# Reordering the first two batches of a linear-attention and swish kernel: fp32 loads of k and q on the hardware queue, one GpSimd queue, and a new order of work around the first Y product

## The chip, the cores and the metric

The kernel runs on one core of a Trainium2 chip. The metric is device time in microseconds (us) of one execution. A core has a matrix engine (TensorE, PE in the profile, with its weight loads listed apart as PEld), a vector engine (VectorE, DVE), an activation engine (ScalarE, ACT), a general engine (GpSimd, POOL) and a queue engine that only issues transfers (SyncE, SP). Each engine runs its own instructions in program order and waits on semaphores for the others. Transfers are issued on SyncE's, ScalarE's or GpSimd's queue; a transfer that changes the type (fp32 in memory to bf16 on chip) is issued by GpSimd.

## The reference

Eight batches of linear attention, then a two-layer feed-forward step over all 4608 rows (8 batches of 576):

```
phi(x) = (x if x > 0 else exp(x) - 1) + 1
kv  = einsum('bhsd,bhse->bhde', phi(k), v)
z   = sum over s of phi(k)
x   = (phi(q) kv) / (phi(q) z + 1e-6)          # (batch, 576, 8 heads * 64)
h   = x @ w_in                                   # 512 -> 2048
g   = h * sigmoid(beta * h)
out = g @ w_out                                  # 2048 -> 512, fp32
```

q, k, v are (8, 8, 576, 64) in fp32, w_in is 512x2048, w_out 2048x512 and beta 2048, all fp32. One batch of q, of k or of v is 1.18 MB, each weight matrix 4.19 MB.

## The kernel before, in words

**The steady part.** From batch 1 on, `h_phase(b)` makes h in 16 blocks of 128 features ("ff"): four 128x512 matmuls (`h_mm`, L334) into one PSUM tile out of four (`mmps`), then one silu on ScalarE (L342) that writes g. `y_phase(b)` multiplies four tiles of 128 rows with w_out (`y_mm`, L352), copies each to SBUF (`y_out`, L364) and stores it. Between the blocks, `at(...)` hangs side work of the next batch on a block's number: `kv_both(n)` (phi(k)^T v, 36 small matmuls, L184), `numer(n, t)` (phi(q) times kv for 128 rows, L285, into the only tile of the pool `numps`, then den, rden and the product xs on VectorE, L293 to L299), and transposes by DMA (`x_trans_dma`, `q_trans_dma`). Products of the last 64 rows of each batch gather in `xT_tail` and are multiplied at the end.

**phi.** `phi_part` takes exp on ScalarE (L149) into a tile "e" that has three buffers; `phi_relu` makes max(x,0)+1 on VectorE (L153) into a tile "r", three buffers too; `phi_min` takes the smaller (L160). Each covers half the heads ("pr" 0 or 1), 1152 columns.

**The first two batches.** The order of work here is written out by hand, and each engine keeps it. Batch 0 has nothing to hide behind: k comes as fp32 by SyncE into `stage`, q and v cast to bf16 by GpSimd; the phi steps are followed by transposes of phi(q) on TensorE (`q_trans0`, copied out of PSUM by ScalarE, through the pool `miscps` with two buffers), `kv_direct` (phi(k)^T v, L195) with its masked copy `kv_evac` (L219), the denominators (`dens`, `recips`, L414 to L422), the products `numer0` (L432) with `norm` (xs, L299), and the transposes `x_trans` (L315) copied into xT by ScalarE (L320) or VectorE (L322). `idle(n)` issues n matmuls on a constant tile. Then come the 16 blocks of h(0), and a stage called Y0 here: the Y product of batch 0, laid between the attention work of batch 1 and the phi of batch 2.

**Weights.** w_in is loaded in four pieces by GpSimd, cast to bf16. w_out is loaded in four fp32 pieces by SyncE into `w_out_f`: pieces 0 and 1 share memory with g of odd batches (`g_sb[1]`, seen as fp32 as `g_f`), pieces 2 and 3 with `stage`, where k of batch 0 lies. `w_out_scale(i, n_act)` (L531 on ScalarE, L533 on VectorE) divides piece i by beta and makes it bf16. `hold(d, after)` makes the issue of one transfer wait until another has landed; pieces 0 and 2 of w_out, k of batch 1 and q of batch 2 are held so.

The lines that matter most for the order are these:

```
e: work.tile(..., tag="e", bufs=3)          # L148
nps: numps.tile(...), pool numps with bufs=1 # L281, L605
y_sb: work.tile(..., tag="y_sb", bufs=3)    # L363
load_w_out(0, w_in_dma[1]); load_w_out(1)    # L119, L120
hold(load(nc.gpsimd, xk[1], k, 1), w_in_dma[3])   # L121
w_out2_dma = load_w_out(2, q1_dma); load_w_out(3) # L458, L459
hold(load(nc.gpsimd, xq[2], q, 2), w_out2_dma)    # L552
```

Of the kernel before, what the change touches and what calls it, by code (L numbers as in the profile page):

```python
# [16 lines left out]
def kernel(  # L17
# [10 lines left out]
    nc = tc.nc  # L28
# [56 lines left out]

    def hold(d, after):
        tc.add_manual_dep(d.ins, after.ins.name, SYNC, reason="share of the queues")


    beta_row = consts.tile([FC, P], F32)  # L90
    for h0 in (0, 2):
        load(nc.sync, k0f, k, 0, h0, 2)
    nc.sync.dma_start(out=beta_row, in_=moe_beta.rearrange("(c p) -> c p", p=P))
    nc.vector.memset(warm, 0.5)  # L94
    tiny = consts.tile([P, 2], BF16)
    nc.scalar.activation(tiny[:, 0:1], warm[:, 0:1], ACTF.Exp)
# [1 line left out]
    make_identity(nc, identity)  # L98
    ident16 = consts.tile([FC, FC], F32)
    make_identity(nc, ident16)  # L100
    for h0 in (0, 2):
        load(nc.gpsimd, xq[0], q, 0, h0, 2)
    for h0 in (0, 2):
        load(nc.gpsimd, vb[0], v, 0, h0, 2)

    w_in_v = moe_w_in.rearrange("(c p) f -> p c f", p=P)
    w_out_v = moe_w_out.rearrange("(c p) m -> p c m", p=P)
    w_in_dma = [
        nc.gpsimd.dma_start(out=w_in_sb[i], in_=w_in_v[:, :, i * 512 : (i + 1) * 512])  # L109
        for i in range(4)  # L110
    ]

    def load_w_out(i, after=None):
        d = nc.sync.dma_start(out=w_out_f[i], in_=w_out_v[:, i * 4 : (i + 1) * 4, :])
        if after is not None:
            hold(d, after)
        return d

    load_w_out(0, w_in_dma[1])  # L119
    load_w_out(1)  # L120
    hold(load(nc.gpsimd, xk[1], k, 1), w_in_dma[3])  # L121
    q1_dma = load(nc.gpsimd, xq[1], q, 1)
    load(nc.gpsimd, vb[1], v, 1)

    kvmask = consts.tile([P, 2, 2, EA], BF16)
    nc.vector.memset(kvmask, 0.0)
    nc.vector.memset(kvmask[:D, :, 0, :], 1.0)
    nc.vector.memset(kvmask[D:P, :, 1, :], 1.0)
    ones = consts.tile([P, 2], BF16)
    nc.vector.memset(ones, 1.0)  # L130
    for i in range(2):
        nc.vector.memset(vaug[i][:, :, :, :, D : D + 2], 1.0)

    warm_ps = mmps.tile([P, 512], F32, tag="mm", name="warm_ps")

# [29 lines left out]
        )  # L165

    def xin(b, a, pr):
        if b == 0 and a == "k":
            return k0f[:, 2 * pr : 2 * pr + 2]
        return (xk if a == "k" else xq)[b % NX][:, 2 * pr : 2 * pr + 2]  # L170

    def v_copy(eng, b, pr):
# [186 lines left out]
    def rows(b, j):  # L359
        return out[b * S : (b + 1) * S, :].rearrange("(g j) m -> j g m", j=J)[j]  # L360

    def y_out(b, t, yp, c0=0, c1=512, queues=(nc.sync, nc.sync)):
        y_sb = work.tile([P, DM], F32, tag="y_sb", name="y_sb", bufs=3)  # L363
        nc.vector.tensor_copy(y_sb[:, c0:c1], yp[:, c0:c1])  # L364
# [77 lines left out]
    def phi_step(a, pr, f, *r):  # L442
        f(0, a, pr, *((xin(0, a, pr),) if f is not phi_min else ()), *r)
# [11 lines left out]
    phi_step("q", 1, phi_part, 0, 4)  # L455
    phi_step("q", 1, phi_part, 4, J)
    phi_step("k", 1, phi_relu)
    w_out2_dma = load_w_out(2, q1_dma)  # L458
    load_w_out(3)  # L459
    phi_step("k", 1, phi_min)  # L460
    zt = [num0_tile() for _ in range(2)]
    z_products(0, 0, zt)
# [9 lines left out]
    z_evac(zt)  # L472
    phi_step("q", 0, phi_min)
    phi_step("q", 1, phi_relu)
    phi_step("q", 1, phi_min, 0, 4)
    phi_step("q", 1, phi_min, 4, J)
    idle(10)

    def q_trans0(t):
        q_trans(0, (t,), misc_bf()[:, 0 : 512 if t < NT - 1 else 256], (nc.scalar,))  # L480

    q_trans0(0)
    q_trans0(1)
    kv_direct(0, 0, kvp0)
    for hh in range(2):
        kv_evac(0, hh, (0,), kvp0)
    q_trans0(2)
    kvp1 = [num0_tile() for _ in range(2)]
    kv_direct(0, 1, kvp1)
    for hh in range(2):  # L490
        kv_evac(0, hh, (1,), kvp1)
    dens(0, (0, 1), dps)
    recips(0, 2, P, dps)
    q_trans0(3)
    numer0(0, 0)
    numer0(0, 1)
# [42 lines left out]
    w_out_scale(0, 0)
    w_out_scale(1, 0)  # L540
    yps = [mm_tile("y_ps") for _ in range(4)]
    phi_all(1, "k")
    phi_all(1, "q")
# [2 lines left out]
            y_mm(0, t, i, yps[t])  # L546
    kv1 = [miscps.tile([P, 512], F32, tag="misc", name="kv1") for _ in range(2)]
    kv_tile(1)
    for pr in range(2):
        z_products(1, pr, kv1)  # L550
    z_evac(kv1)
    hold(load(nc.gpsimd, xq[2], q, 2), w_out2_dma)  # L552
    load(nc.gpsimd, xk[2], k, 2)
    load(nc.gpsimd, vb[0], v, 2)

    for ts in ((0, 1), (2, 3)):
        q_trans(1, ts, num0_tile().bitcast(BF16), (nc.scalar, nc.scalar))
    for pr in range(2):
        kv_direct(1, pr, kv1)
    w_out_scale(2, 0)  # L560
    for hh in range(2):
        kv_evac(1, hh, (0, 1), kv1)
    dps1 = num0_tile()
    q_trans(1, (4,), dps1.bitcast(BF16)[:, 512:768], (nc.scalar,))
    y_mm(0, 0, 2, yps[0])
# [17 lines left out]
    y_mm(0, 1, 3, yps[1])
    y_out(0, 1, yps[1])
    x_trans(1, 3, nc.vector)
    phi_tile(2, "q")
    phi_tile(2, "k")
# [4 lines left out]
    phi_min(2, "q", 0)
    phi_part(2, "k", 0, xin(2, "k", 0))
    y_mm(0, 2, 3, yps[2])
    y_out(0, 2, yps[2])
    phi_min(2, "q", 1)
    phi_part(2, "k", 1, xin(2, "k", 1))
    y_mm(0, 3, 3, yps[3])
    y_out(0, 3, yps[3])
# [89 lines left out]
```

## Time and profile before

| quantity | value |
|---|---|
| time, median of 10 runs | 295.49 us (294.22 to 296.24) |
| the profiled execution's own time | 295.46 us |
| its span (first to last instruction) | 293.7 us |
| TensorE busy | 284.9 us (97%) |
| ScalarE busy | 159.9 us (54%) |
| VectorE busy | 116.5 us (40%) |
| GpSimd busy | 33.7 us (11%) |
| HBM read, written | 36.71 MB, 9.44 MB |

The span leaves out 1.8 us around it, in which the execution starts and ends. The busy share of TensorE is high for a reason beside useful work: matmuls are pipelined and their ends are modelled, and the `idle` matmuls count too. So the gaps of an engine, and who ended them, say more than its share. In the views, a line begins with the start in us and the duration in us, then engine, line, operation, output<-input, and, in brackets, how long the engine had been idle and what ended the idle time.

### The profile page before, as it was taken

Reading aid. Unit: us, or ns where it says so; the run is one execution under the profiler, and the core shown is the slowest. Engines: PE = TensorE matmul, PEld = TensorE weight load, DVE = VectorE, ACT = ScalarE, POOL = GpSimd, SP = SyncE. Lnnn points to the kernel's source line nnn. Section 1 sums busy time; section 2 is a strip of 40 time slices with the busy share of each in tenths; the row PEclk is TensorE's granted clock in tenths of the full one; section 3 lists DMA queues with packets and bytes.
Section 4 is the critical chain, followed back from the end, with each engine's and each line's share of the span. In section 5 each row is a group of like instructions: output and inputs, shape, how many; then the busy total and the mean of one; then the engine's idle time right before and its main releaser. Section 6 shows DMA issues by size and latency. Waiting matters only on the chain.

```text
span 293.7 us, 4697 instructions
## 1 busy us (share of the span) xinstructions
PE 284.9 (97%) x1853; PEld 143.0 (49%) x1881; DVE 116.5 (40%) x266; ACT 159.9 (54%) x208; POOL 33.7 (11%) x50
## 2 busy tenths in 40 slices
PE   8999999999999999999999999999999999999995
PEld 3584456445445444554455445544554444444443
DVE  4753478843724461356135622653251200110012
ACT  5658956855936772678157906690661077018500
POOL 9103020320050005000500053000000000000000
PEclk9999999999999999999999999999999999999999
DMA  7999989789389859952993299416131310131032
GB/s 202 202 213 329 195 291 197 191 250 189 73 223 261 111 53 212 281 85 59 238 250 73 50 234 255 91 35 164 38 71 44 73 37 0 36 74 36 0 71 73
DMA packets 51910, 40.82 MB, mean 139 GB/s; under 512 B 30752, under 2 KB 42288, under 8 KB 51888
## 3 DMA queue, kind: packets, MB, share of 16 engines
q1 hardware_dynamic: 40080, 27.68, 37.2%
q0 software_dynamic: 11648, 12.72, 26.4%
q8 instruction: 14, 0.23, 0.3%
q10 hardware_dynamic: 160, 0.13, 0.2%
q14 instruction: 8, 0.07, 0.1%
HBM read 36.71 MB, written 9.44 MB: 157 GB/s over the span
## 4 chain that ended last, share of the span: by engine, by line
PE 79%; DMA 12%; POOL 2%; DVE 2%; issue 1%; ACT 1%; SPq 0%; POOLq 0%
PE y_ps L352 39%; PE h_ps L334 35%; DMA w_in<-in_moe_w_in_dram 6%; DMA xq<-in_q_dram 3%; PE nps L285 3%; DMA stage<-in_moe_w_out_dram 2%; PE kvp L184 2%; DMA qTd<-phi_q 1%; POOL w_in L109 1%; ACT g L342 1%; POOL xq L81 1%; DVE w_out L533 1%; POOL vf L81 0%; PE nps L432 0%; ACT L342 0%
## 5 line engine op out<-in xcount | busy, mean ns | idle before, releaser
L342 ACT ACTIVATE g<-h_ps,beta_c 128x512 bf16<-128x512 f32 x144 | 98.0, 688 | 100.6 <-PE h_ps L334 100.4
L352 PE MATMUL y_ps<-w_out,g 128*128 128x512 bf16 (+2 forms) x581 | 126.7, 373 | 1.0 <-DVE w_out L533 0.2
L334 PE MATMUL h_ps<-xT,w_in 128*128 128x512 bf16 (+1 forms) x545 | 116.7, 360 | 1.0 <-DVE y_sb L364 0.4
L352 PEld LDWEIGHTS <-g 128*128 128x128 bf16 x592 | 57.4, 98 | 65.7 <-issue 0.8
L334 PEld LDWEIGHTS <-w_in 128*128 128x128 bf16 x624 | 56.6, 98 | 58.9 <-issue 1.0
L364 DVE COPY y_sb<-y_ps 128x512 f32<-128x512 f32 (+2 forms) x37 | 24.9, 675 | 84.5 <-PE y_ps L352 80.9
L299 DVE TENSOR_TENSOR xs<-nps,rden 128x512 bf16<-128x512 f32 (+1 forms) x40 | 27.2, 687 | 4.8 <-DMA xT<-xs 2.4
L81 POOL DMA_DIRECT2D xk<-in_k_dram x7 | 5.4, 771 | 118.7 <-DMA qTd<-phi_q 77.5
L149 ACT ACTIVATE e<-xq 128x1152 bf16<-128x1152 bf16 (+2 forms) x17 | 17.9, 1099 | 1.8 <-DMA xq<-in_q_dram 1.7
L160 DVE TENSOR_TENSOR phi_q<-e,r 128x1152 bf16<-128x1152 bf16 (+2 forms) x17 | 12.2, 722 | 15.9 <-ACT e L149 15.8
L149 ACT ACTIVATE e<-xk 128x1152 bf16<-128x1152 bf16 x14 | 15.5, 1151 | 1.2 <-DVE phi_q L160 1.1
L234 DVE TENSOR_TENSOR kv_bd<-kvp,kvmask 128x260 bf16<-128x260 f32 x12 | 4.6, 424 | 25.8 <-PE kvp L184 25.8
L293 DVE TENSOR_SCALAR den<-nps 128x8 f32<-128x8 f32 (+1 forms) x30 | 5.0, 165 | 23.4 <-PE nps L285 23.4
L334 PE MATMUL h_ps<-xT_tail,w_in 128*128 128x512 bf16 x63 | 13.9, 379 | 0.1
L285 PEld LDWEIGHTS <-qTd 128*128 128x128 bf16 x120 | 9.4, 98 | 7.9 <-DMA qTd<-phi_q 0.8
L160 DVE TENSOR_TENSOR phi_k<-e,r 128x1152 bf16<-128x1152 bf16 x16 | 11.6, 753 | 3.8 <-ACT e L149 3.8
L285 PE MATMUL nps<-kv_bd,qTd 128*128 128x130 bf16 x120 | 12.1, 221 | 1.0 <-DMA qTd<-phi_q 0.6
L174 POOL CAST vaug<-vf 128x1152 bf16<-128x1152 f32 x10 | 11.2, 1161 | 3.6 <-DMA vf<-in_v_dram 3.6
L138 PE MATMUL warm_ps<-warm 128*128 128x512 bf16 x27 | 8.7, 483 | 1.6 <-DVE warm L94 1.5
L149 ACT ACT_TABLE_LOAD x6 | 7.7, 1283 | 2.8 <-DMA xq<-in_q_dram 2.7
L342 ACT ACT_TABLE_LOAD x7 | 9.0, 1283 | 0.1
L81 POOL DMA_DIRECT2D xq<-in_q_dram x9 | 6.8, 755 | 14.5 <-DMA stage<-in_moe_w_out_dram 14.5
(67 smaller groups left out, 104.2 us busy)
## 6 DMA issues: line engine op xcount, KB each, us to landing
out_dram<-y_sb SPq DMA_DIRECT2D x70, 128.0 KB, 2.4
vf<-in_v_dram SPq DMA_DIRECT2D x5, 1152.0 KB, 7.6
xk<-in_k_dram POOLq DMA_DIRECT2D x7, 576.0 KB, 8.6
xq<-in_q_dram POOLq DMA_DIRECT2D x7, 576.0 KB, 12.7
w_in<-in_moe_w_in_dram POOLq DMA_DIRECT2D x4, 512.0 KB, 13.4
g<-in_moe_w_out_dram SPq DMA_DIRECT2D x2, 1024.0 KB, 9.5
stage<-in_moe_w_out_dram SPq DMA_DIRECT2D x2, 1024.0 KB, 7.7
stage<-in_k_dram SPq DMA_DIRECT2D x2, 576.0 KB, 4.3
```

The lines of the kernel that those rows point to most:

```text
L81: return eng.dma_start(out=dst[:, h0 : h0 + n].rearrange("p h j d -> p h (j d)"), in_=rows.rearrange("(i p) e -> p i e", p=P)[:, h0 : h0 + n],
L138: nc.tensor.matmul(warm_ps[:, 0:cols], warm[:, 0:P], warm[:, 0:cols], start=True, stop=True)
L149: nc.scalar.activation(st[b, a, pr, "e"][:, :, j0:j1], x[:, :, j0:j1], ACTF.Exp)
L160: nc.vector.tensor_tensor(st[b, a][:, pr, j0:j1].rearrange("p j (h d) -> p j h d", h=2), st[b, a, pr, "e"][:, :, j0:j1].rearrange("p h j d ...
L174: eng.tensor_copy(vaug[b % 2][:, pr, :, :, 0:D], src[:, 2 * pr : 2 * pr + 2].rearrange("p h j d -> p j h d"),)
L184: nc.tensor.matmul(ps[hh, pr], st[b, "k"][r, pr, j, :], vaug[b % 2][r, pr, j, :, 0:EA], start=(j == 0), stop=(j == J - 1), skip_group_chec ...
L285: nc.tensor.matmul(nps[: qs.shape[-1], hh, pr * 2 * EA : (pr + 1) * 2 * EA], qs, st[b, "kv"][:, hh, pr, :], start=True, stop=True, skip_gr ...
L299: nc.vector.tensor_mul(xs[:n].rearrange("p i a d -> p a i d"), num, rd[:, :, :, None].to_broadcast([n, 2, 4, D]),)
L334: nc.tensor.matmul(hp[:, c0:c1], w_in_sb[ff // 4][:, kc, (ff % 4) * P : (ff % 4 + 1) * P], x[:, kc, c0:c1], start=(kc == 0), stop=(kc == K ...
L342: nc.scalar.activation(g_sb[b % 2][:, ff, :], hp, ACTF.Silu, scale=beta_c[:, ff : ff + 1])
L352: nc.tensor.matmul(yp[:, c0:c1], g_sb[b % 2][:, ff, t * P : (t + 1) * P], w_out_sb[i][:, c, c0:c1], start=(ff == 0), stop=(ff == FC - 1), ...
L364: nc.vector.tensor_copy(y_sb[:, c0:c1], yp[:, c0:c1])
```

## The change

- **Loads of batch 0.** q of batch 0 now comes as fp32 by SyncE behind k, into `g_sb[1]` (`q0f`); its phi reads fp32. beta is issued by ScalarE. v of batch 0 is issued by GpSimd once the first half of k has landed.
- **One GpSimd queue.** All w_out pieces move from SyncE's queue to GpSimd's. The order there is v of batch 0, w_in 0 to 3, w_out 0 to 2, k and q of batch 1, w_out 3, v of batch 1, then q, k, v of batch 2. The four holds named above are gone. The memsets of `kvmask` move from VectorE to GpSimd.
- **Batch 0.** `q_trans0(2)` comes before the first `kv_direct`; `dens` and `recips` of tiles 0 and 1 come before the second.
- **Y0.** The part of w_out piece 2 (`y_mm(0, t, 2)`) is spread between the sums z and the transposes of q of batch 1. Piece 3 of w_out is scaled on VectorE alone, earlier. The copy of y tile 0 goes to ScalarE; the copies of y tiles 1, 2, 3 go behind the last `norm` of batch 1. The exps of q of batch 2 move forward, the other phi steps of batch 2 come after the y copies. `x_trans(1, 1)` is copied by VectorE.
- **h(1).** `x_trans(1, 4)` moves from block 0 to block 5, `kv_both(2)` from 6 to 8; `numer(2, t)` moves from blocks 7, 9, 11, 13, 15 to blocks 10, 11, 12, 13, 14.

```diff
+    q0f = g_f[:, 0 : 4 * J * D].rearrange("p (h j d) -> p h j d", h=4, j=J)
...
-    for h0 in (0, 2):
-        load(nc.sync, k0f, k, 0, h0, 2)
-    nc.sync.dma_start(out=beta_row, in_=moe_beta.rearrange("(c p) -> c p", p=P))
+    nc.scalar.dma_start(out=beta_row, in_=moe_beta.rearrange("(c p) -> c p", p=P))
+    k0_dma, _, _, _ = [
+        load(nc.sync, dst, src, 0, h0, 2) for dst, src in ((k0f, k), (q0f, q)) for h0 in (0, 2)
+    ]
...
-    for h0 in (0, 2):
-        load(nc.gpsimd, xq[0], q, 0, h0, 2)
-    for h0 in (0, 2):
-        load(nc.gpsimd, vb[0], v, 0, h0, 2)
...
-    load_w_out(0, w_in_dma[1])
-    load_w_out(1)
-    hold(load(nc.gpsimd, xk[1], k, 1), w_in_dma[3])
-    q1_dma = load(nc.gpsimd, xq[1], q, 1)
-    load(nc.gpsimd, vb[1], v, 1)
-
-    nc.vector.memset(kvmask, 0.0)
-    nc.vector.memset(kvmask[:D, :, 0, :], 1.0)
-    nc.vector.memset(kvmask[D:P, :, 1, :], 1.0)
+    nc.gpsimd.memset(kvmask, 0.0)
+    nc.gpsimd.memset(kvmask[:D, :, 0, :], 1.0)
+    nc.gpsimd.memset(kvmask[D:P, :, 1, :], 1.0)
...
+    for h0 in (0, 2):
+        hold(load(nc.gpsimd, vb[0], v, 0, h0, 2), k0_dma)
+    for i in range(4):
+        nc.gpsimd.dma_start(out=w_in_sb[i], in_=w_in_v[:, :, i * 512 : (i + 1) * 512])
+    def load_w_out(i):
+        nc.gpsimd.dma_start(out=w_out_f[i], in_=w_out_v[:, i * 4 : (i + 1) * 4, :])
...
-    w_out2_dma = load_w_out(2, q1_dma)
-    load_w_out(3)
...
     phi_step("q", 1, phi_relu)
+    for i in range(3):
+        load_w_out(i)
+    load(nc.gpsimd, xk[1], k, 1)
+    load(nc.gpsimd, xq[1], q, 1)
+    load_w_out(3)
+    load(nc.gpsimd, vb[1], v, 1)
...
-    q_trans0(0)
-    q_trans0(1)
+    for t in range(3):
+        q_trans0(t)
     kv_direct(0, 0, kvp0)
     for hh in range(2):
         kv_evac(0, hh, (0,), kvp0)
-    q_trans0(2)
+    dens(0, (0, 1), dps)
+    recips(0, 2, P, dps)
     kvp1 = [num0_tile() for _ in range(2)]
     kv_direct(0, 1, kvp1)
     for hh in range(2):
         kv_evac(0, hh, (1,), kvp1)
-    dens(0, (0, 1), dps)
-    recips(0, 2, P, dps)
...
+    load(nc.gpsimd, xq[2], q, 2)
+    load(nc.gpsimd, xk[2], k, 2)
+    load(nc.gpsimd, vb[0], v, 2)
     nc.vector.reciprocal(rbeta, beta_c)
-    w_out_scale(0, 0)
-    w_out_scale(1, 0)
+    for i in range(3):
+        w_out_scale(i, 0)
...
     kv_tile(1)
+    y_mm(0, 0, 2, yps[0])
     for pr in range(2):
         z_products(1, pr, kv1)
     z_evac(kv1)
+    w_out_scale(3, 0)
     for ts in ((0, 1), (2, 3)):
         q_trans(1, ts, num0_tile().bitcast(BF16), (nc.scalar, nc.scalar))
+    y_mm(0, 1, 2, yps[1])
+    y_mm(0, 2, 2, yps[2])
+    dps1 = num0_tile()
+    q_trans(1, (4,), dps1.bitcast(BF16)[:, 512:768], (nc.scalar,))
     for pr in range(2):
         kv_direct(1, pr, kv1)
...
+    y_mm(0, 3, 2, yps[3])
+    y_mm(0, 0, 3, yps[0])
+    y_out(0, 0, yps[0], copier=nc.scalar)
     numer0(1, 0)
     numer0(1, 1)
+    phi_tile(2, "q")
+    phi_tile(2, "k")
+    phi_part(2, "q", 0, xin(2, "q", 0))
+    y_mm(0, 1, 3, yps[1])
     x_trans(1, 0, nc.scalar)
     numer0(1, 2)
+    phi_part(2, "q", 1, xin(2, "q", 1))
+    y_mm(0, 2, 3, yps[2], 0, 256)
+    x_trans(1, 1, nc.vector)
     numer0(1, 3)
+    y_mm(0, 2, 3, yps[2], 256, 512)
+    y_mm(0, 3, 3, yps[3], 0, 256)
     x_trans(1, 2, nc.vector)
+    y_mm(0, 3, 3, yps[3], 256, 512)
+    x_trans(1, 3, nc.vector)
     numer0(1, 4)
+    for t in (1, 2, 3):
+        y_out(0, t, yps[t])
     for pr in range(2):
+        phi_part(2, "k", pr, xin(2, "k", pr))
+        phi_relu(2, "q", pr, xin(2, "q", pr))
+        phi_min(2, "q", pr)
     for pr in range(2):
         phi_relu(2, "k", pr, xin(2, "k", pr))
...
         if b == 1:
-            at(sh, 0, lambda: q_trans_dma(2), lambda: x_trans(1, 4, nc.vector))
+            at(sh, 0, lambda: q_trans_dma(2))
+            at(sh, 5, lambda: x_trans(1, 4, nc.vector))
...
-            at(sh, 6 if b == 1 else 4, lambda: kv_both(n))
+            at(sh, 8 if b == 1 else 4, lambda: kv_both(n))
             for t in range(NT):
-                at(sh, (7 if b == 1 else 5) + 2 * t, lambda t=t: numer(n, t))
-                at(sh, min((8 if b == 1 else 6) + 2 * t, FC - 1), lambda t=t: x_trans_dma(n, t))
+                ff = 10 + t if b == 1 else 5 + 2 * t
+                at(sh, ff, lambda t=t: numer(n, t))
+                at(sh, ff + 1, lambda t=t: x_trans_dma(n, t))
```

More of the change, by code (lines that the diff above doesn't have):

```diff
@@ L100 @@
     make_identity(nc, ident16)
-    for h0 in (0, 2):
-        load(nc.gpsimd, xq[0], q, 0, h0, 2)
-    for h0 in (0, 2):
-        load(nc.gpsimd, vb[0], v, 0, h0, 2)
[L106 to L117, printed above, removed]
-    load_w_out(0, w_in_dma[1])
-    load_w_out(1)
-    hold(load(nc.gpsimd, xk[1], k, 1), w_in_dma[3])
-    q1_dma = load(nc.gpsimd, xq[1], q, 1)
-    load(nc.gpsimd, vb[1], v, 1)
     kvmask = consts.tile([P, 2, 2, EA], BF16)
-    nc.vector.memset(kvmask, 0.0)
-    nc.vector.memset(kvmask[:D, :, 0, :], 1.0)
-    nc.vector.memset(kvmask[D:P, :, 1, :], 1.0)
+    nc.gpsimd.memset(kvmask, 0.0)
+    nc.gpsimd.memset(kvmask[:D, :, 0, :], 1.0)
+    nc.gpsimd.memset(kvmask[D:P, :, 1, :], 1.0)
     ones = consts.tile([P, 2], BF16)
@@ L132 @@
         nc.vector.memset(vaug[i][:, :, :, :, D : D + 2], 1.0)
+    for h0 in (0, 2):
+        hold(load(nc.gpsimd, vb[0], v, 0, h0, 2), k0_dma)
+    w_in_v = moe_w_in.rearrange("(c p) f -> p c f", p=P)
+    w_out_v = moe_w_out.rearrange("(c p) m -> p c m", p=P)
+    for i in range(4):
+        nc.gpsimd.dma_start(out=w_in_sb[i], in_=w_in_v[:, :, i * 512 : (i + 1) * 512])
+    def load_w_out(i):
+        nc.gpsimd.dma_start(out=w_out_f[i], in_=w_out_v[:, i * 4 : (i + 1) * 4, :])
     warm_ps = mmps.tile([P, 512], F32, tag="mm", name="warm_ps")
@@ L167, in xin @@
     def xin(b, a, pr):
-        if b == 0 and a == "k":
-            return k0f[:, 2 * pr : 2 * pr + 2]
+        if b == 0:
+            return (k0f if a == "k" else q0f)[:, 2 * pr : 2 * pr + 2]
         return (xk if a == "k" else xq)[b % NX][:, 2 * pr : 2 * pr + 2]
@@ L360, in rows, with y_out @@
         return out[b * S : (b + 1) * S, :].rearrange("(g j) m -> j g m", j=J)[j]
-    def y_out(b, t, yp, c0=0, c1=512, queues=(nc.sync, nc.sync)):
+    def y_out(b, t, yp, c0=0, c1=512, queues=(nc.sync, nc.sync), copier=nc.vector):
         y_sb = work.tile([P, DM], F32, tag="y_sb", name="y_sb", bufs=3)
-        nc.vector.tensor_copy(y_sb[:, c0:c1], yp[:, c0:c1])
+        copy(copier, y_sb[:, c0:c1], yp[:, c0:c1])
         for i in range(2):
@@ L551 @@
     z_evac(kv1)
-    hold(load(nc.gpsimd, xq[2], q, 2), w_out2_dma)
-    load(nc.gpsimd, xk[2], k, 2)
-    load(nc.gpsimd, vb[0], v, 2)
+    w_out_scale(3, 0)
     for ts in ((0, 1), (2, 3)):
         q_trans(1, ts, num0_tile().bitcast(BF16), (nc.scalar, nc.scalar))
+    y_mm(0, 1, 2, yps[1])
+    y_mm(0, 2, 2, yps[2])
+    dps1 = num0_tile()
+    q_trans(1, (4,), dps1.bitcast(BF16)[:, 512:768], (nc.scalar,))
     for pr in range(2):
         kv_direct(1, pr, kv1)
[L560 to L565, printed above, removed]
     dens(1, range(NT), dps1)
@@ L568 @@
     recips(4, 5, G, dps1)
-    y_mm(0, 1, 2, yps[1])
+    for hh in range(2):
+        kv_evac(1, hh, (0, 1), kv1)
+    y_mm(0, 3, 2, yps[3])
+    y_mm(0, 0, 3, yps[0])
+    y_out(0, 0, yps[0], copier=nc.scalar)
     numer0(1, 0)
     numer0(1, 1)
-    w_out_scale(3, 2)
-    y_mm(0, 2, 2, yps[2])
+    phi_tile(2, "q")
+    phi_tile(2, "k")
+    phi_part(2, "q", 0, xin(2, "q", 0))
+    y_mm(0, 1, 3, yps[1])
     x_trans(1, 0, nc.scalar)
     numer0(1, 2)
-    y_mm(0, 3, 2, yps[3])
-    x_trans(1, 1, nc.scalar)
+    phi_part(2, "q", 1, xin(2, "q", 1))
+    y_mm(0, 2, 3, yps[2], 0, 256)
+    x_trans(1, 1, nc.vector)
     numer0(1, 3)
-    y_mm(0, 0, 3, yps[0])
-    y_out(0, 0, yps[0])
+    y_mm(0, 2, 3, yps[2], 256, 512)
+    y_mm(0, 3, 3, yps[3], 0, 256)
     x_trans(1, 2, nc.vector)
+    y_mm(0, 3, 3, yps[3], 256, 512)
+    x_trans(1, 3, nc.vector)
     numer0(1, 4)
[L583 to L587, printed above, removed]
+    for t in (1, 2, 3):
+        y_out(0, t, yps[t])
     for pr in range(2):
-        phi_part(2, "q", pr, xin(2, "q", pr))
-    for pr in range(2):
+        phi_part(2, "k", pr, xin(2, "k", pr))
         phi_relu(2, "q", pr, xin(2, "q", pr))
[L592 to L599, printed above, removed]
+        phi_min(2, "q", pr)
     for pr in range(2):
```

## The prediction

> **What bounds the kernel now.** I read the chain of waits first, then TensorE's timeline for gaps, then the timelines of the engines that end the gaps, then the transfers stretch by stretch. The page gives the shares of busy time and of the chain:
>
> ```profile
> PE 284.9 (97%) x1853; PEld 143.0 (49%) x1881; DVE 116.5 (40%) x266; ACT 159.9 (54%) x208; POOL 33.7 (11%) x50
> PE 79%; DMA 12%; POOL 2%; DVE 2%; issue 1%; ACT 1%; SPq 0%; POOLq 0%
> ```
>
> The chain puts 12% on transfers, all before 62.5 us, so this looks transfer-bound at the front. TensorE's timeline denies it from 16.5 us on: h(0), Y0 and h(1) follow one another with gaps below 0.7 us. I cut the front into stages. Up to 16.54 us (first h0 matmul) VectorE's chain rules; 16.5 to 32.08 is h(0); 32.08 to 52.53 is Y0; 52.53 to 70.53 is h(1) with attention of batch 2. From 70.5 us nothing in the diff touches the program. The hand-over from Y0 to h(1) in ScalarE's timeline is the part to know by heart:
>
> ```profile
> 50.94 1.16 ACT L149 ACTIVATE e<-xk 128x1152 bf16<-128x1152 bf16 x1
> 53.24 1.16 ACT L149 ACTIVATE e<-xk 128x1152 bf16<-128x1152 bf16 x1 [1.15 <-DVE phi_q L160]
> 54.43 1.28 ACT L342 ACT_TABLE_LOAD   x1
> 55.72 3.82 ACT L342 ACTIVATE g<-h_ps,beta_c 128x512 bf16<-128x512 f32 x6
> ```
>
> The fourth exp of batch 2 waited for phi_q: there are three buffers "e", and the fourth tile takes the one that the first `phi_min` has read. Table load and first silu of h(1) stand behind that exp. VectorE's timeline shows how early that min came, with only one y copy between the copy of xT and the relus:
>
> ```profile
> 50.78 0.69 DVE L364 COPY y_sb<-y_ps 128x512 f32<-128x512 f32 x1
> 51.39 0.41 DVE L322 COPY xT<-xtp 128x512 bf16<-128x512 bf16 x1
> 51.73 0.82 DVE L153 TENSOR_SCALAR r<-xq 128x1152 bf16<-128x1152 bf16 x2
> 52.46 0.75 DVE L160 TENSOR_TENSOR phi_q<-e,r 128x1152 bf16<-128x1152 bf16 x1
> ```
>
> And one `numer` of h(1), VectorE's timeline:
>
> ```profile
> 62.89 0.17 DVE L293 TENSOR_SCALAR den<-nps 128x8 f32<-128x8 f32 x1 [1.25 <-PE nps L285]
> 63.09 0.20 DVE L294 RECIPROCAL rden<-den 128x8 f32<-128x8 f32 x1
> 63.33 0.69 DVE L299 TENSOR_TENSOR xs<-nps,rden 128x512 bf16<-128x512 f32 x1
> 64.84 0.17 DVE L293 TENSOR_SCALAR den<-nps 128x8 f32<-128x8 f32 x1 [0.83 <-PE nps L285]
> ```
>
> TensorE ended that product at 62.85; xs ended at 64.02. So the only nps tile is taken for 1.2 us, and the 0.83 us idle shows slack at a distance of two blocks.
>
> **What the Trainium skill says.** "DMA: Bandwidth & Descriptors", section Anatomy of one DMA, prices a GpSimd-issued load at about 2.0 us + bytes/436e3: 2.4 us of moving for a w_out piece (estimate). The trace moves w_in at 205 to 209 GB/s written as bf16, so some 410 read: near it; an fp32-to-fp32 load on that queue is not in it. The same page, section Queues, rings and completion order, has each transfer engine serve its rings in turn. The trace differs; in the stretch 23 to 24 us, with both queues loaded (packets, MB, share):
>
> ```profile
> q1 hardware_dynamic: 176, 0.36, 97.0%
> q0 software_dynamic: 17, 0.02, 9.7%
> ```
>
> The hardware queue took nearly all. "ScalarE: Activation LUTs", section What ACT_TABLE_LOAD costs, gives 1283 ns and a drain of about 1380 ns; the trace shows 1283 ns and the silu 10 ns later, so I charge 1.28.
>
> **Loads.** k and q by SyncE: 2.36 MB at 0.40 MB/us (394 to 406 GB/s at 3 to 5 us), 0.28 of it moved by 3.0 us: ends near 8.2, where q ended at 10.18 before. v is held until 4.46 (first half of k landed), but GpSimd's transfers got almost nothing before 5.4 us anyway: free. Then one queue at 0.41: v and w_in 5.37 MB end at 21.3; w_out 0 to 2 at 29.0; k1 31.9; q1 34.8; w_out 3 37.3; v1 40.2; q2 43.1; k2 46.0; v2 48.8 (before 54.5). GpSimd issues 0.75 us each, two v, four w_in, then w_out from about 11 us when phi has read q0f: always ahead of the queue. Moving the issues off SyncE leaves it only stores. ScalarE's beta issue costs 0.46 us as SyncE's row did, ahead of a table load that ended 2.2 us before the first exp could start; GpSimd's kvmask memsets (0.62 us on VectorE, 0.2 each by GpSimd's own memset rows) lie before k lands. Both cost nothing; past 2.2 us they would delay the first exp or v.
>
> **Ramp.** VectorE works from 4.46 almost unbroken: r(k), min, r(k), min 8.1, beta 8.8. fp32 makes each r(q) 0.76 us (row of `stage`) in place of 0.45: +0.6, which the two waits for exps (0.56 at 9.9 and 0.1 at 11.1) absorb because q is early. Last min of q about 11.95; before 11.97. So the earlier q buys nothing. `q_trans0(2)` now waits in front of `kv_direct` for ScalarE's first copy (two misc buffers; copy 0.58 from 11.9), so `kv_direct` starts 0.5 us later, half of it regained by `dens` running in its shadow: **+0.25**. Bounds: -1.0 (VectorE follows q) to +0.6. h(0) is TensorE's own; Y0 starts at 32.3.
>
> **Y0.** TensorE's sum for the same instructions: 64 y matmuls 13.9, z 0.54, 18 transposes 1.0, kv 1.1, dens 0.6, 20 numer 1.17, 16 transposes 0.9: 19.2 us. Before took 20.45. The new order puts y blocks before each product that waits: w_out 3 lands at 37.3, needed by VectorE near 40.8; v1 at 40.2, needed near 43.4; q2 before 47.6. I keep 0.4 for the last xT copy and small waits: h(1) starts at T = 32.3 + 19.6 = **51.9** (gain 0.6). A transfer over 3 us late reaches TensorE.
>
> **Hand-over.** VectorE after T: norm of tile 4 ends T+0.6; three y copies, 0.62 each: T+2.5; r(q) 0.41, min 0.75: T+3.65. Only then exp k1 (T+3.7 to 4.85), table 1.28, silu 0.69: T+6.85. TensorE has four PSUM tiles: blocks 0 to 3 at 0.864, block 1 waiting 0.45 for y copy 1, end at T+3.9. Block 4 waits for silu 0: **a stall of 2.95 us**, starting block 4 at 58.75. Before, block 3 started at 56.06, block 4 at 56.92. Behind the waiting exp stand table and all silus; behind the y copies all phi of batch 2. qTd (issue after min q1 at about T+4.9, some 6 us to the second landing) comes by 63 and is needed at 66.
>
> **Rest of h(1).** Before, block 4 to the end: 70.53 - 56.92 = 13.61. To add: `x_trans(1,4)` 0.22, now after block 4. The numers stand one block apart: 0.864 us for a tile taken 1.2: stall 0.36, four times, **+1.43**. To subtract: the qTd wait 0.64. Gives 14.62, end at 73.37 against 70.53: +2.84. The profiled 295.46 becomes **298.3**; the median (295.49) is the same within 0.03.
>
> **Rivals.**
> - *Half the loss (12%).* One of the two stalls is hidden: without the nps waits 296.9, without the hand-over's 295.4. Speaks for it that y tile 1 is ready by 48 us; against it that VectorE keeps program order, and that before's exp did wait 1.15 us for its tile. Mostly 296 to 297.
> - *Late transfers (15%).* w_out on GpSimd's queue is unmeasured. Below: at 0.436 MB/us all is 2 us earlier, worth nothing. Above: at half speed each piece costs 2.6 more, v1 lands at 50.6, 7 us after need: 305. At 0.33 MB/us v1 lands near 48 if everything slows (5 us late), at 42.7 if only w_out does: nothing. Value taken: 0.41. Typical of this case: 300 to 303.
> - *The front was transfer-bound (8%), not slower.* The chain's 12% is right, q's 1.9 us and the earlier weights pull the start of h(0). It decides when T is below 49.1: 2.84 earlier than mine. For it: the chain; against: VectorE busy 7.49 of 10 us at 10 to 20, TensorE without gaps after 16.5. T of 48.5 gives 294.9.
>
> **Numbers.** Main case 65%, its own range 297.2 to 299.8; a measurement tells about 0.2% (0.6 us) from no change. Half: 3 of 12 within 0.2%, the rest slower; front: 6 of 8 faster, 2 same. Faster 0.06, same 0.05, slower 0.89. Range 295.9 to 301.8: leaves out the front case and late transfers of the heavy kind.
>
> **To look for after.** ScalarE's fourth exp of batch 2 with a wait of over 3 us for phi_q; the first silu of h(1) near 58; TensorE idle near 3 us before block 4; nps waits of 0.3 to 0.4 for xs, four times; no wait for q at VectorE before 12 us; w_out transfers at about 400 GB/s on the software queue. I am wrong if h(1) starts before 50, if the exp finds a free tile, or if TensorE waits for a transfer in Y0.

## The result, and the profile after

The changed kernel takes 301.41 us (median of 9 runs, 299.73 to 301.79) against 295.21 for the kernel before (32 runs): a ratio of 1.0192, with a 95% interval of 1.0170 to 1.0214. The forecast was slower, 298.3 in a range of 295.9 to 301.8. The direction and the two main waits came as forecast; the size is twice the forecast.

The profiled execution after took 299.73 us with a span of 298.0 (before 295.46 and 293.7), so the profile shows 4.3 us of the loss. The page's shares hardly move; in the chain that ended last the share of transfers falls from 12% to 2%, and TensorE's grows from 79% to 90%:

```profile
PE 285.1 (96%) x1860; PEld 143.6 (48%) x1889; DVE 116.8 (39%) x265; ACT 158.3 (53%) x206; POOL 35.8 (12%) x55
PE 90%; DVE 4%; DMA 2%; ACT 2%; issue 1%; SPq 0%; DVEq 0%
```

By the stages of the forecast, read from TensorE's timeline (us from the start of the span):

| point | before | after | difference grows by |
|---|---|---|---|
| h(0) starts | 16.54 | 17.32 | +0.78 |
| Y0 starts | 32.08 | 32.75 | -0.11 |
| h(1) starts | 52.53 | 52.65 | -0.55 |
| block 4 of h(1) starts | 56.92 | 59.48 | +2.44 |
| Y phase of batch 1 starts | 70.53 | 74.73 | +1.64 |
| end of the span | 293.7 | 298.0 | +0.1 |

**The hand-over.** ScalarE's timeline after, the same four instructions as before:

```profile
50.84 1.15 ACT L138 ACTIVATE e<-xk 128x1152 bf16<-128x1152 bf16 x1
56.27 1.16 ACT L138 ACTIVATE e<-xk 128x1152 bf16<-128x1152 bf16 x1 [4.27 <-DVE phi_q L149]
57.45 1.28 ACT L331 ACT_TABLE_LOAD   x1
58.74 3.58 ACT L331 ACTIVATE g<-h_ps,beta_c 128x512 bf16<-128x512 f32 x6
```

The exp's wait for its buffer has grown from 1.15 to 4.27 us, because on VectorE the three y copies now stand ahead of the first min of q:

```profile
52.53 0.68 DVE L288 TENSOR_TENSOR xs<-nps,rden 64x512 bf16<-64x512 f32 x1
53.13 1.87 DVE L231 COPY y_sb<-y_ps 128x512 f32<-128x512 f32 x3
54.93 0.44 DVE L142 TENSOR_SCALAR r<-xq 128x1152 bf16<-128x1152 bf16 x1
55.47 0.76 DVE L149 TENSOR_TENSOR phi_q<-e,r 128x1152 bf16<-128x1152 bf16 x1
```

TensorE's timeline shows what that costs, and the distance of the numer products. First the kernel before, at block 3 and at two of the numer products:

```profile
56.06 3.61 PE L334 MATMUL h_ps<-xT,w_in 128*128 128x512 bf16 x16 [0.45 <-DVE y_sb L364]
...
64.65 1.89 PE L334 MATMUL h_ps<-xT,w_in 128*128 128x512 bf16 x8
66.37 0.40 PE L285 MATMUL nps<-kv_bd,qTd 128*128 128x130 bf16 x4
```

Then the changed kernel:

```profile
53.86 2.75 PE L323 MATMUL h_ps<-xT,w_in 128*128 128x512 bf16 x12 [0.18 <-DVE y_sb L231]
59.48 1.89 PE L323 MATMUL h_ps<-xT,w_in 128*128 128x512 bf16 x8 [2.87 <-ACT g L331]
...
67.35 1.02 PE L323 MATMUL h_ps<-xT,w_in 128*128 128x512 bf16 x4
68.73 0.41 PE L274 MATMUL nps<-kv_bd,qTd 128*128 128x130 bf16 x4 [0.36 <-DVE xs L288]
```

That is 2.87 us of idling before block 4, and 0.36 us before each of four numer products. The five products stand 1.63 us apart (67.11, 68.73, 70.37, 72.00, 73.63), where their own work and one block take 0.23 + 0.864 us in a row without waits: each wait costs 0.54 us, the idle time and 0.18 more. Most of the 0.18 is seen in the block ahead of the wait: it lasts 1.02 us to its (modelled) end, where in an unbroken row the next work starts 0.864 us after it. This part is called the refill below.

**What the profile doesn't show.** The mean granted clock is the share of full speed that TensorE's clock was let run at, averaged over an execution. Of the ten executions of the changed kernel with a clock on record, four took 299.73 to 300.47 us at a mean granted clock of 0.997 to 0.999, and six 301.41 to 301.79 at 0.992 to 0.994. The profiled one is of the first group, the median of the second: 1.7 us that no view of that profile holds. Runs e1 and e5 below point to where it is lost.

### The profile page after: what moved, and what is told of

Its sections match the earlier page's. It is cut to its first block, busy times and chain, and to the rows that moved or that the text cites. A ratio compares the mean times of both kernels' runs of the same rounds, so it can differ in the third digit from the quotient of the medians.

```text
span 298.0 us, 4712 instructions
## 1 busy us (share of the span) xinstructions
PE 285.1 (96%) x1860; PEld 143.6 (48%) x1889; DVE 116.8 (39%) x265; ACT 158.3 (53%) x206; POOL 35.8 (12%) x55
## 3 DMA queue, kind: packets, MB, share of 16 engines
q1 hardware_dynamic: 38480, 24.65, 34.4%
## 4 chain that ended last, share of the span: by engine, by line
PE 90%; DVE 4%; DMA 2%; ACT 2%; issue 1%; SPq 0%; DVEq 0%
PE y_ps L341 42%; PE h_ps L323 39%; PE nps L274 3%; PE kvp L173 2%; DMA g<-in_q_dram 2%; DVE xs L288 1%; PE nps L421 1%; ACT e L138 1%; PE xtp L304 1%; DVE y_sb L231 1%; DVE phi_q L149 1%; PE kv L184 1%; ACT g L331 0%; ACT L331 0%; PE nps L242 0%
## 5 line engine op out<-in xcount | busy, mean ns | idle before, releaser
L341 PE MATMUL y_ps<-w_out,g 128*128 128x512 bf16 (+3 forms) x588 | 125.9, 370 | 0.8 <-issue 0.2
L341 PEld LDWEIGHTS <-g 128*128 128x128 bf16 x600 | 58.2, 98 | 65.4
L231 DVE COPY y_sb<-y_ps 128x512 f32<-128x512 f32 (+2 forms) x36 | 24.1, 673 | 85.8 <-PE y_ps L341 83.1
L138 ACT ACTIVATE e<-xq 128x1152 bf16<-128x1152 bf16 x14 | 15.6, 1156 | 0.1
L173 PEld LDWEIGHTS <-phi_k 64*128 64x128 bf16 x216 | 6.3, 94 | 2.5 <-issue 2.5
```

Of the source, the lines that this page charges most:

```text
L138: nc.scalar.activation(st[b, a, pr, "e"][:, :, j0:j1], x[:, :, j0:j1], ACTF.Exp)
L173: nc.tensor.matmul(ps[hh, pr], st[b, "k"][r, pr, j, :], vaug[b % 2][r, pr, j, :, 0:EA], start=(j == 0), stop=(j == J - 1), skip_group_chec ...
L231: eng.tensor_copy(dst, src)
L341: nc.tensor.matmul(yp[:, c0:c1], g_sb[b % 2][:, ff, t * P : (t + 1) * P], w_out_sb[i][:, c, c0:c1], start=(ff == 0), stop=(ff == FC - 1), ...
```

## The experiments

Theory A: the loss is made of TensorE's waits at three hand-overs (exp for its buffer, one nps tile, TensorE's order in the ramp). The rivals (clock, transfers, ramp by transfers) stand in the expectations. The spans are those of each kernel's profiled execution, the ratios are to the kernel before on the same chip.

**e1_space: the numer products two blocks apart again.**

```diff
-            at(sh, 8 if b == 1 else 4, lambda: kv_both(n))
+            at(sh, 6 if b == 1 else 4, lambda: kv_both(n))
-                ff = 10 + t if b == 1 else 5 + 2 * t
+                ff = 7 + 2 * t if b == 1 else 5 + 2 * t
...
```

> The changed kernel with the products numer(2, t) of h(1) put back two blocks apart (blocks 7 to 15) and kv_both back to block 6; all else as changed. Theory A (the loss is three hand-overs inside the front: exp waiting for its buffer, one nps tile at one-block distance, TensorE's order in the ramp): the four waits of TensorE for xs vanish, h(1) ends 2.1 us sooner than in the changed kernel (4 x 0.54, the distance of two numers less 0.864 and 0.23), so the span falls from 298.0 to about 295.9. Rival B (the loss is a lower granted clock or late transfers): span within 0.5 us of 298.0. If the qTd transposes land after block 7 then up to 0.5 us of it is lost again.

Measured: 299.56 us, ratio 1.0123 (1.0082 to 1.0164), and the waits for xs are gone. But the profiled span is 298.2, not 295.9. Two things stand against the saved 2.1 us. Y0 started 0.74 us later in this execution (33.49; the second half of k landed later, and VectorE waited for it), and after the 2.87 us wait TensorE's matmuls took twice as long. The timeline around block 4, then the clock column (the third from the right) in stretches of 1 us (1.00 is full speed):

```profile
60.22 2.84 PE L323 MATMUL h_ps<-xT,w_in 128*128 128x512 bf16 x8 [2.87 <-ACT g L331]
```

```profile
60.00:61.00 1.00, 0.78 (x4) 0.39 (x4) 0.28 (x1) 1.00 (x3) 0.00 (x0) 1.00 0.66 170
61.00:62.00 1.00, 1.00 (x4) 0.30 (x2) 0.00 (x0) 1.00 (x3) 0.00 (x0) 0.50 0.84 196
62.00:63.00 1.00, 1.00 (x4) 0.16 (x2) 0.00 (x0) 0.48 (x1) 0.00 (x0) 0.50 0.87 179
63.00:64.00 1.00, 1.00 (x7) 0.51 (x7) 0.29 (x1) 0.69 (x1) 0.00 (x0) 0.50 0.83 191
64.00:65.00 1.00, 1.00 (x11) 0.35 (x10) 0.00 (x0) 0.09 (x1) 0.91 (x2) 0.80 0.98 366
```

Eight matmuls took 2.84 us where the changed kernel's profile has 1.89 for them. The clock is granted at half from 61.0 us, 0.8 us after TensorE resumed, to about 64.3 us: some 3.4 us, in which half of the work is lost. That is 1.7 us, the distance of the two groups of executions, and it would lower the mean clock of a span of 298 us by 0.006, as the groups show. Here they lie at 297.8 and 297.94 (clock 1.0) and at 299.31 to 299.96 (0.991 to 0.994). The undisturbed executions are 2.2 us below those of the changed kernel, as theory A has it; and rival B is half right, since a lower clock is part of the loss.

**e5_fill: TensorE kept busy in the wait.**

```diff
+            at(sh, 3, lambda: fill(12))
...
+    def fill(n):
+        fp = miscps.tile([P, 512], F32, tag="misc", name="fill_ps")
+        for _ in range(n):
+            nc.tensor.matmul(fp, warm[:, 0:P], warm, start=True, stop=True)
```

> The changed kernel with 12 matmuls on a constant tile (128x512, into a free PSUM tile, never read) between blocks 3 and 4 of h(1), where TensorE otherwise waits 2.87 us for the first silu. They take 2.6 us and delay nothing. Theory D (in most executions of the changed kernel TensorE's clock is halved for some 3.7 us after that wait, which costs 1.7 us on top of the wait): with TensorE busy the clock stays whole, all executions lie at 299.7 to 300.5 us, none at 301.4 and above; the span is 298.0. Rival E (the spread of 299.7 to 301.8 has nothing to do with the wait): the median stays near 301.4.

Measured: 300.01 us; six executions, all between 299.85 and 300.12, clock 0.998 to 1.0; span 298.2. TensorE's timeline:

```profile
56.65 2.75 PE L599 MATMUL fill_ps<-warm 128*128 128x512 bf16 x12
59.68 1.89 PE L323 MATMUL h_ps<-xT,w_in 128*128 128x512 bf16 x8 [0.28 <-ACT g L331]
```

Useless matmuls in the wait make the kernel faster by 1.4 us in the median, with no instruction of the path moved. None of the six has a low clock, where six of ten had one without the fill. So the half clock is a consequence of TensorE idling there, as theory D has it; six executions can't exclude that it still comes now and then. The wait itself is still paid: the ratio is 1.0154 (1.0114 to 1.0194).

**e2_etile: a free tile for the fourth exp.**

```diff
+            if (b, a, pr) == (2, "k", 1):
+                st[b, a, pr, "e"] = xk[0][:, 0:2]
+            else:
                 st[b, a, pr, "e"] = work.tile([P, 2, J, D], BF16, tag="e", name="e", bufs=3)
```

> The changed kernel with one edit: the fourth exp of batch 2 (k, second half) writes into xk[0], which lies unused then, in place of the third-from-last e buffer; nothing else moves. Theory A: the exp starts near 52.0 right behind the third, the first silu of h(1) near 54.5, TensorE's idle before block 4 falls from 2.87 us to under 0.3, span about 295.2 (2.8 us less). Rival B: the exp moves but the span stays within 0.5 us of 298.0, since something else ends as late.

Measured: 296.97 us (296.76 to 297.45, 12 runs), ratio 1.0054 (1.0035 to 1.0073), span 295.1. ScalarE's timeline:

```profile
52.10 1.15 ACT L141 ACTIVATE xk<-xk 128x1152 bf16<-128x1152 bf16 x1
53.27 1.28 ACT L334 ACT_TABLE_LOAD   x1
54.56 1.26 ACT L334 ACTIVATE g<-h_ps,beta_c 128x512 bf16<-128x512 f32 x2
```

One tile moved, and the silu comes 4.2 us sooner, TensorE's wait before block 4 is gone, the span is 2.9 us shorter, and the time 4.4 us: the wait and the half clock together. This one buffer is over two thirds of the loss.

**e3_ramp: batch 0's order of before.**

```diff
-    for t in range(3):
-        q_trans0(t)
+    q_trans0(0)
+    q_trans0(1)
     kv_direct(0, 0, kvp0)
     ...
-    dens(0, (0, 1), dps)
-    recips(0, 2, P, dps)
+    q_trans0(2)
     ...
+    dens(0, (0, 1), dps)
+    recips(0, 2, P, dps)
```

> The changed kernel with only batch 0's order put back: q_trans0(2) after the first kv_direct, dens and recips of tiles 0 and 1 after the second. Theory A: TensorE's order cost the ramp 0.7 us, so h(0) starts near 16.6 in place of 17.3 and the span is about 297.3. Rival C (the ramp is late by its transfers: v or the second half of q arrive late): h(0) still starts near 17.3 and kv_direct is seen waiting for v.

Measured: 300.56 us, ratio 1.0174 (1.0136 to 1.0212), span 297.5; h(0) starts at 16.65, and the first `kv_direct` at 12.15 in place of 12.86 without a wait for v. The span is 0.5 us shorter; the difference of the ratios is within their intervals, since three of the six executions have the low clock. The profiles are clearer. In the changed kernel TensorE's timeline reads:

```profile
11.59 0.51 PE L242 MATMUL tp<-identity,phi_q 128*128 128x128 bf16 x6 [0.43 <-DVE phi_q L149]
12.55 0.38 PE L242 MATMUL tp<-identity,phi_q 128*128 128x128 bf16 x4 [0.45 <-ACT qT L229]
12.86 0.68 PE L184 MATMUL kvp<-vf,phi_k 64*128 64x128 bf16 x18
13.47 0.35 PE L403 MATMUL dps<-z,qT 128*128 128x2 bf16 x8
13.76 0.68 PE L184 MATMUL nps<-vf,phi_k 64*128 64x128 bf16 x18
...
17.32 1.05 PE L323 MATMUL h_ps<-xT,w_in 128*128 128x128 bf16 x16
```

And in e3:

```profile
11.71 0.51 PE L242 MATMUL tp<-identity,phi_q 128*128 128x128 bf16 x6 [0.47 <-DVE phi_q L149]
12.15 0.68 PE L184 MATMUL kvp<-vf,phi_k 64*128 64x128 bf16 x18
12.76 0.40 PE L242 MATMUL tp<-identity,phi_q 128*128 128x128 bf16 x4
13.09 0.68 PE L184 MATMUL nps<-vf,phi_k 64*128 64x128 bf16 x18
...
16.65 1.05 PE L323 MATMUL h_ps<-xT,w_in 128*128 128x128 bf16 x16
```

The third transpose waits for ScalarE's copy and holds `kv_direct`; then `dens` stands ahead of the second `kv_direct`, on which all numer0 products wait. From the first line of each block (TensorE released by VectorE's min of q) to h(0) it takes 5.73 or 5.74 us in every profile with the changed order (after, e1, e2, e5, e11), and 4.94 or 4.95 with before's order (before, e3, e6, e8, e9, e10; e4 5.25, with a wait of 0.25 us for v). So the order costs 0.79 us of the ramp; 0.68 is left when Y0 starts. What else moves the ramp is when k lands, which differs between executions of one program: e11 and e1 started h(0) 0.8 and 0.7 us later than the profile after, for that reason. Rival C, as a cause of the 0.78 us, is out.

**e4_all: the three edits together (e1, e2, e3).**

> The changed kernel with all three put back or mended (numer two blocks apart, the fourth exp in xk[0], batch 0's old order). Theory A with the parts independent: 298.0 - 2.1 - 2.8 - 0.7 = 292.4, that is 1.3 us below the span before (293.7). But h(1) then reaches block 7 near 60.5 and the qTd transposes land at about 62.5, so about 1.5 us come back as a wait for them: about 294. Rival B: above 296.

Measured: 295.75 us (22 runs), ratio 1.0026 (1.0013 to 1.0039), span 293.9. It is what the expectation names after its sum: the parts come back but for TensorE's wait for the qTd transposes at block 7.

```profile
62.70 0.29 PE L277 MATMUL nps<-kv_bd,qTd 128*128 128x130 bf16 x2 [0.75 <-DMA qTd<-phi_q]
```

So the changed kernel, without its three waits, is still 0.26% slower than before, and its new loads and Y0 order bring no gain on top.

**e6_loads: only the loads, in before's order of computation.** The part of the edit that moves w_out and batch 1:

```diff
-    load_w_out(0, w_in_dma[1])
-    load_w_out(1)
...
     phi_step("q", 1, phi_relu)
+    for i in range(3):
+        load_w_out(i)
+    load(nc.gpsimd, xk[1], k, 1)
+    load(nc.gpsimd, xq[1], q, 1)
+    load_w_out(3)
+    load(nc.gpsimd, vb[1], v, 1)
...
```

> The kernel before with only the loads of the change: k and q of batch 0 as fp32 by SyncE, beta by ScalarE, v held for k, all w_out and later loads on GpSimd's queue in the changed order, kvmask by GpSimd; all computation in the order of before. The forecast's step (loads arrive earlier, and nobody on the path waits for them): within 0.6 us of before, with h(0) starting at 16.5 to 17.0. Rival (the front was transfer-bound): 1 to 2 us faster, w_out 2 and 3 scaled without a wait. Other rival (the single queue makes things late): VectorE waits for w_out or ScalarE for k of batch 1, and Y0 is longer than 20.45 us.

Measured: 297.10 us (20 runs), ratio 1.0060 (1.0041 to 1.0078); h(0) starts at 16.79, but Y0 takes 22.0 us (32.34 to 54.34). TensorE's timeline there:

```profile
40.84 0.28 PE L241 MATMUL nps<-identity,phi_q 128*128 128x128 bf16 x2 [0.90 <-DVE phi_q L148]
41.54 0.96 PE L241 MATMUL nps<-identity,phi_q 128*128 128x128 bf16 x14 [0.42 <-DVE phi_q L148]
43.21 1.18 PE L183 MATMUL kv<-vf,phi_k 64*128 64x128 bf16 x36 [0.71 <-DVE w_out L525]
```

k of batch 1 came behind three pieces of w_out, so ScalarE began its exps at 36.4 us (before 34.3) and phi(q) ended late; the weight loads for `kv_direct` sat 0.9 us until v landed, as the waits from 38 to 44 us have it (the bracket of the last line above names only what came last by the profile):

```profile
PEld L183 <- DMA vf<-in_v_dram: 0.9, 1, 0.9
```

The third reading of the expectation is right: the single queue made things late, and in before's order somebody on the path waits for it. Part of the median is clock: seven of the 20 executions have a mean clock of 0.994 or less; the other 13 have a median of 296.81 us, 1.5 above before, about as much as Y0 grew. In the changed kernel the same lateness is there (k of batch 1 at 34.4 us; exps at 35.8) and TensorE does not wait for it: a y block now stands in front of z and the transposes. That this block is the reason is argued from the order, not tried alone.

**e7_space: only the places in h(1), in the kernel before.**

```diff
-            at(sh, 6 if b == 1 else 4, lambda: kv_both(n))
+            at(sh, 8 if b == 1 else 4, lambda: kv_both(n))
-                at(sh, (7 if b == 1 else 5) + 2 * t, lambda t=t: numer(n, t))
+                ff = 10 + t if b == 1 else 5 + 2 * t
+                at(sh, ff, lambda t=t: numer(n, t))
...
```

> The kernel before with only the change's places in h(1): kv_both at block 8, the five numer products at blocks 10 to 14, transposes behind them. Theory A: four waits of TensorE for xs, each 0.36 us of idling and 0.18 us of refilling, 2.15 us in all, less the 0.8 us that the wait for qTd at block 7 costs before: 1.3 us slower (span about 295.0). If only the idle time counts, 0.6 us slower.

Measured: 296.83 us (20 runs), ratio 1.0050 (1.0031 to 1.0070). In the profiled execution h(1) takes 19.14 us (51.94 to 71.08) against 18.0 before, +1.1 of the 1.3 expected; its span is only 294.2, since its Y0 ended 0.6 us sooner. The four waits of 0.36 us are there; the first of them:

```profile
63.69 1.02 PE L334 MATMUL h_ps<-xT,w_in 128*128 128x512 bf16 x4
65.08 0.41 PE L285 MATMUL nps<-kv_bd,qTd 128*128 128x130 bf16 x4 [0.36 <-DVE xs L299]
```

The refill counts: with the idle time alone (four times 0.36, less the 0.8 of the wait for qTd that falls away) h(1) would have grown by only 0.6 us.

**e11_split: one y copy behind the min.**

```diff
-    for t in (1, 2, 3):
+    for t in (1, 2):
         y_out(0, t, yps[t])
...
         phi_min(2, "q", pr)
+        if pr == 0:
+            y_out(0, 3, yps[3])
```

> The changed kernel with the copy of y tile 3 behind the first phi_min of q of batch 2 in place of ahead of it. The hand-over chain is one copy (0.62 us) shorter and TensorE's wait of 2.87 us falls into two: 0.7 us before block 3 (for the copy) and 1.7 us before block 4 (for the silu). Theory A: span 297.4. Theory D (the long unbroken wait halves the clock): with 1.7 us as the longest wait all executions keep the clock, times of 299.0 to 299.6, none 1.5 us above. Rival: the clock falls as often as in the changed kernel, so that it is the sum of the waits that counts, not the longest.

Measured: 299.53 us, ratio 1.0134 (1.0107 to 1.0162). From the start of h(1) to block 4 it takes 6.23 us (after: 6.83), 0.60 less as expected, with waits of 0.55 and 1.55 us:

```profile
57.11 1.04 PE L323 MATMUL h_ps<-xT,w_in 128*128 128x512 bf16 x4 [0.55 <-DVE y_sb L231]
59.70 1.89 PE L323 MATMUL h_ps<-xT,w_in 128*128 128x512 bf16 x8 [1.55 <-ACT g L331]
```

The span, 298.2, hides the gain: in this execution the first half of k landed 0.9 us later than in the profile after, and Y0 started at 33.56 in place of 32.75. Five of six executions lie at 299.16 to 299.95 with a clock of 0.998 to 1.0, one at 301.19 with 0.993. So the expectation's theory D, by which a longest wait of 1.55 us leaves every execution its clock, failed in one of six; whether the low clock is rarer than in the changed kernel (six of ten) is not shown by so few.

**Where else the low clock appears.** Counting executions with a mean clock of 0.994 or less, beside the waits of TensorE in each profile after 16 us:

| kernel | executions with 0.994 or less | longest waits of TensorE, us |
|---|---|---|
| after, e1, e3 | 13 of 22 | 2.87 |
| e8 | 4 of 16 | 1.94 |
| e11 | 1 of 6 | 0.55 and 1.55 within 3.2 us |
| e6 | 7 of 20 | 0.90, 0.42 and 0.71 within 3.3 us |
| e7 | 2 of 20 | 0.36, four times |
| before (beside all experiments) | 5 of 129 | 0.64 |
| e2, e4, e5, e9, e10 | 0 of 82 | 0.75 (e4) |

So the long wait is not the only road to a low clock: e6 has no wait of 1 us, but three that make up 2.0 of 3.3 us. That fits a limit on the idle share of a stretch better than one on a single wait. It is not shown: the one kept trace with a half clock inside the work is e1's, and where the clock fell in the other executions is not on record.

**e8_best and e9_best2: the repaired kernel with the numer products later.** Both are e4 with `kv_both` at block 8, numer at 9, 11, 13, 15 and the fifth in the Y phase; e9 moves phi of q of batch 3 behind that one.

```diff
-                ff = 7 + 2 * t if b == 1 else 5 + 2 * t
-                at(sh, ff, lambda t=t: numer(n, t))
-                at(sh, min(ff + 1, FC - 1), lambda t=t: x_trans_dma(n, t))
+                ff = 9 + 2 * t if b == 1 else 5 + 2 * t
+                if ff < FC:
+                    at(sh, ff, lambda t=t: numer(n, t))
+                    at(sh, min(ff + 1, FC - 1), lambda t=t: x_trans_dma(n, t))
+                else:
+                    at(sy, 1, lambda t=t: numer(n, t), lambda t=t: x_trans_dma(n, t))
...
-            at(sy, 0, lambda: phi_all(m, "q"))
+            at(sy, 1 if b == 1 else 0, lambda: phi_all(m, "q"))     # e9 alone
```

> The changed kernel with the fourth exp in xk[0], batch 0's order of before, and the numer products of batch 2 two blocks apart but later: kv_both at block 8, numer at 9, 11, 13, 15 and the last one after the second group of matmuls in the Y phase of batch 1. Theory A: no wait for xs, none for qTd, none of ScalarE for the buffer. Against the all-mended kernel (span 293.9, which waited 0.8 us for qTd): 293.0 to 293.2, that is 0.5 to 0.7 us below before. Rival: the moved product stalls the Y phase, or the ramp eats it: 293.7 or more.

> The kernel of run e8_best with one mend: the phi of q of batch 3 now stands behind the last numer of batch 2 (both after the second group of matmuls of the Y phase), so that VectorE does not wait for q of batch 3 before it takes that product. In e8 the product's xs came at 79.1 us behind a wait for q, and with it the stores on SyncE's queue and TensorE's 1.9 us before block 4 of h(2). If that was the cause the 2.1 us of waits of TensorE for y copies fall to under 0.3 and the span to 293.0 to 293.4; if the Y phase has no room for the product, the wait stays above 1 us.

Measured: e8 297.72 us, ratio 1.0080 (1.0056 to 1.0105): a miss. h(1) itself went as hoped, but VectorE took the fifth product only behind the relu of q of batch 3, which waited 3.93 us for its transfer, and TensorE lost 1.94 us in h(2) to a late y copy:

```profile
74.43 0.83 DVE L145 TENSOR_SCALAR r<-xq 128x1152 bf16<-128x1152 bf16 x2 [3.93 <-DMA xq<-in_q_dram]
...
87.92 1.89 PE L326 MATMUL h_ps<-xT,w_in 128*128 128x512 bf16 x8 [1.94 <-DVE y_sb L234]
```

e9, with the order mended: 294.98 us (20 runs), ratio 0.9983 (0.9969 to 0.9998), span 292.4, no wait above 0.4 us in h(1). It is below the kernel before by 0.17%, and the interval only just leaves out no change.

**e10_before_late: the same places in the kernel before, nothing else of the change.**

> The kernel before with only the places in h(1) changed, to a distance of two blocks but later than before: kv_both at block 8, numer at 9, 11, 13, 15 and the last in the Y phase, phi of q of batch 3 behind it. Theory A: no wait for the transposes of q (0.64 us and some 0.28 of refill before) and none for xs: span 0.9 us less than before, 292.8. Rival: within 0.3 us of before, since the moved product costs the Y phase as much.

Measured: 294.62 us (22 runs), ratio 0.9977 (0.9961 to 0.9993), span 292.4. The first numer no longer waits for qTd; before, and in e10:

```profile
62.56 0.29 PE L285 MATMUL nps<-kv_bd,qTd 128*128 128x130 bf16 x2 [0.64 <-DMA qTd<-phi_q]
62.13 0.40 PE L285 MATMUL nps<-kv_bd,qTd 128*128 128x130 bf16 x4
```

That is a gain of 0.7 us by the ratio (0.9 forecast for the span), and as good as e9: the loads and the Y0 order of the change are not needed for it.

## Why the forecast was right, and where it was not

- **The number: in part luck.** 301.41 lies inside the range, 0.4 us from its end, but above the main case's own 297.2 to 299.8. It falls where the forecast saw late transfers (300 to 303), and those did not come: TensorE waits for no transfer in the profile after. The cause was the main case's; its price was too low.
- **Hand-over: right.** Forecast T+6.85 us from the start of h(1) to block 4 and a stall of 2.95; measured 6.83 and 2.87. e2 shows the buffer as its cause.
- **The step that failed: the sum as a whole was taken over to the median ("the median (295.49) is the same within 0.03").** It priced the stall as its own length. In six of ten executions the time is 1.7 us longer: e1's trace shows TensorE's clock halved behind the stall, and with the stall filled no execution is so long (e5). This is the larger part of the missing 3.1 us. The other 1.4 stand in the profile: h(1) started at 52.65 and not 51.9, and from block 4 on it took 0.63 us more than forecast. The Trainium skill's page "TensorE: Matmul & The Clock Gate", section Part 1: The HAM clock gate, states it: half clock after an idle window of about 3.4 us, the window running freely. The 3.4 us of half clock in e1 agree with its window. The wait does not: a wholly idle stretch of 3.4 us does not fit into 2.87 us, and yet the low clock came in most executions. So here less than a whole window of idling was enough. A free-running window would explain why not in every execution, but no run separates that from other causes.
- **nps: mechanism and idle time right (0.36 us, four times), size wrong.** The term 1.43 measures 2.15, for the refill of 0.18 us that each wait adds.
- **Ramp: wrong.** Forecast +0.25, measured +0.78 (in the profiles the changed order costs 0.79, see e3). The step "half of it regained by `dens` running in its shadow" was false: `dens` stands ahead of the second `kv_direct` on TensorE, and that decides when numer0 starts. VectorE's last min of q ended at 11.94 us, forecast 11.95: that the change to q's load buys nothing was right, but not for the stated reason. q was hardly earlier (its exps started at 8.38 and 9.89 us, before at 8.68 and 10.18), and the longer r(q) took the 0.3 us back; that the two figures meet is in part luck.
- **Y0: right in length (19.9 us, forecast 19.6), by partly wrong arrivals.** q's second half landed at 9.89 us, not 8.2, since the hardware queue moved 311 to 366 GB/s from 5 to 8 us and not 400; k of batch 1 came at 34.4, not 31.9. The slack in Y0 covered it; e6 shows what the loads cost in before's order (1.8 us). That they cost nothing held only together with the Y0 order that came with them.
- **Rivals.** The transfer-bound front is out: the new loads alone slow the kernel (e6), and h(1) started at 52.65 us, not before 49.1. Late transfers are out, as said above. The half-loss case is out, both waits are there. w_out on GpSimd's queue ran at 389 to 401 GB/s (23 to 29 us), near the 410 taken.

## What to carry to other kernels

Before moving an instruction ahead of another on a busy engine, look for the buffer that the second one frees, and follow it to the end: here three copies of 0.62 us held one exp, its table load, all silus and TensorE. Price a wait of TensorE by more than its idle time: add the refill, and ask whether the clock falls behind it. No run here finds a length below which it is safe: one wait of 2.87 us was enough in most executions, and e6 lost clock with waits of 0.90 us at most. A single profile can miss that; compare the clock and the spread of all executions.

## What was not expected of the hardware

- In e1's trace TensorE's clock was granted at 0.50 for about 3.4 us, from 0.8 us after the end of a wait of 2.87 us. The mean clock was as low in 13 of 22 executions with that wait (six of ten of the changed kernel), and in none of the six of e5, with 12 useless matmuls in the wait.
- A wait of 0.36 us between matmuls cost 0.54 us, four times in the changed kernel.
- In the changed kernel GpSimd, with ten loads issued by 14.6 us, waited for an older one to land before most further issues (q of batch 1 at 15.74 us, 1.18 us of waiting for a piece of w_in). The queue never ran dry for it; whether the program's semaphores or the queue set this limit was not tried.
